# An order change at a stage border: the flip of token tile 15 directly behind that of tile 14, the first right side's differences and parts ahead of the second sums

## The chip, the cores and the metric

The kernel runs on one core of one Trainium2 chip. The metric is device time in microseconds (us), the median of several executions. Smaller is better.

## What is computed

A transformer block with adaptive layer norm, one sequence of 2048 tokens, width 512, all in float32:

```python
mod = (_silu(c) @ w_mod).reshape(c.shape[0], 6, 1, -1)
sa, ca, ga, sb, cb, gb = (mod[:, 0], mod[:, 1], mod[:, 2], mod[:, 3], mod[:, 4], mod[:, 5])
h = _layernorm(x, axis=-1) * (1 + ca) + sa
x = x + ga * _A_ref(h, A_wqkv, A_wo)
h = _layernorm(x, axis=-1) * (1 + cb) + sb
x = x + gb * _B_ref(h, B_w_gate, B_w_up, B_w_down)
```

`_A_ref` is linear attention with 32 heads of 16. `_B_ref` is a feed-forward part, `((x @ w_gate) * (x @ w_up)) @ w_down`, with 1376 hidden columns, worked on in 11 tiles of up to 128.

## The kernel before, in words

**Precision.** Each matmul operand is split into a high part (a ScalarE copy to fp32r) and a low part (the operand minus its high part, on VectorE or GpSimd). A product is three matmuls: high by high, high by low, low by high (`product` L205, `times` L1021). So every operand has to pass two engines before TensorE can use both of its parts.

**Tiles.** The 2048 tokens are 16 token tiles of 128 rows, in four chunks of four. In the attention's last part, `y_a(i)` (L748) multiplies the transposed queries of tile i with the output weights in 12 matmuls, on top of a residual that `y_seed(i)` (L740) has put into the accumulator bank `acc`, and `y_b(i)` (L757) takes the bank out on ScalarE (L763) and measures its mean and variance on VectorE (L229, L230). Two accumulator banks take turns (`y_bank`), so the seed of tile 15 waits for the statistics of tile 13.

Tiles 8 to 15 are transposed on the way through DRAM: `move_out` and `move_in` (DMA L709, L717) shift whole blocks, and `turn_v(i)` (L719) flips the 32x32 blocks on VectorE (L722, "the flip"). `turn_h(i)` (L674) makes the high part on ScalarE (L676), `turn_l(i)` (L678) the low part on VectorE (L680).

**The second stage.** The larger part of the feed-forward work uses a recursive product with seven half-size products in place of eight. For two chunks and one column tile, `block` (L1044) issues the seven products `times` of six matmuls each, into four banks a, b, c, d. In the order of TensorE: a = a11·b11; ScalarE copies a to b (`copy(b, a)`, L1031); d = s1·t1; b += s2·t2; a += a12·b21; ScalarE copies b to c; c += s3·t3; d += s4·b22; c += a22·t4. Here the left sides are token data: sums and differences s1 to s4 (`Left.sum`, L944 on GpSimd), split by `Left.split` (high L196 on ScalarE, low L197 on VectorE), once for each of k = 0 and k = 1 (`first[0]`, `first[1]`). The right sides are weights: `right_sums` makes the four differences t1 to t4 (L994), `right_split` makes the high parts on ScalarE (L1005 for b11, then L1008 for t1 and t2 together, for t3 and t4, for b21 and b22) and the low parts on GpSimd (L1012, in the same order).

**What sets the order.** Nothing reorders the program. `manual_schedule` keeps each engine's queue as the calls stand in the source, so every engine works through its list and waits in place for what its next instruction needs. SBUF tiles come out of a pool of 94 buffers; a new tile may wait for the last user of the buffer that it gets.

**The border between the stages.** The calls that the change moves stand at L1317 to L1332. Before them GpSimd makes the sums of `first[1]`. Behind them the first block begins: `work = ffn()`, then `y_step(14)` issues `y_a(14)`; `fill(1)` issues the first piece of block 0 (a and the copy); `y_b(14)`, `right_sums(1)` on VectorE and the splits of s3, s4 follow between the pieces d, and b and a; then comes `y_step(15)` with `y_a(15)`. `take()` is the adding of the last `down` pass to the residual (L824 on VectorE, twice).

Of the kernel before, what the change touches and what calls it, by code (L numbers as in the profile page):

```python
# [24 lines left out]
def tile_adaln_block(  # L25
# [12 lines left out]
    nc = tc.nc  # L38
# [31 lines left out]
    def f32(ap):  # L70
        return ap.bitcast(F32)
# [7 lines left out]
    def B(tag, shape=(P, D), dt=F32):  # L79

        return T(tiles, tag, shape, dt)
# [4 lines left out]
    def bank():  # L86
        return T(ps_w, "bank")
# [586 lines left out]
    def turn_h(i):  # L674
        pqs[i] = (B("xh", dt=F32R), B("xl", dt=F32R))
        nc.scalar.activation(pqs[i][0], tps[i], AF.Copy)  # L676

    def turn_l(i):  # L678
        h, l = pqs[i]
        nc.vector.tensor_tensor(l, tps.pop(i), f32(h), op=ALU.subtract)  # L680
# [38 lines left out]
    def turn_v(i):  # L719

        tps[i] = B("f")
        nc.vector.transpose(tps[i].rearrange("p (s m i) -> p m s i", m=NQ, i=BL),  # L722
                            moved.pop(i).rearrange("p (m i s) -> p m s i", m=NQ, i=BL))
# [16 lines left out]
    def y_seed(i, of=acc_bank):  # L740

        yps[i] = of()
        if of is bank:

            nc.tensor.matmul(yps[i], wp[0][0][:, :P], wp[0][0], start=True, stop=True)
        nc.scalar.activation(yps[i], xts[i // NJ][i % NJ], AF.Copy)
# [10 lines left out]
    def y_b(i):  # L757
        ch, j = divmod(i, NJ)
        ps = yps.pop(i)
        if ch in SUMS:  # L760
            norm2[ch].stats_act(j, ps)
            return
        nc.scalar.activation(xts[ch][j], ps, AF.Copy)  # L763
        norm2[ch].stats(j, of=ps)
# [372 lines left out]
    def right_sums(n, on=None):  # L1137
        if n < len(steps):
            rights[n].sums(on)

    def right_split(n, on=None):
        if n < len(steps):
            rights[n].high()
            rights[n].lows(on)
# [3 lines left out]
    def draw_load(n):  # L1148
        if n < len(steps):
            f0, k = fts[steps[n][1]]  # L1150
            draws[n] = load(w_down[f0:f0 + k, :], "raw")

    banks = []
# [120 lines left out]
    first = [Left((0, 1), k).into(side) for k in range(KH)]  # L1274
# [42 lines left out]
    first[1].sum("s1", "s3", "s2", "s4", on=nc.gpsimd)  # L1317
    y_seed(14, y_bank)
    turn_h(14)
    first[0].split("s1", "s2")  # L1320
    turn_l(14)
    y_b(13)
    y_seed(15, y_bank)
    right_sums(0, nc.vector)
    take()
    first[1].split("s1", "s2")
    turn_v(15)
    for n in range(4):
        banks.append(bank())
    banks[:] = [banks[n] for n in (2, 0, 1, 3)]  # L1330
    turn_bank[0] = acc_bank
    right_split(0)  # L1332
    draw_load(0)
    stash, second_side, plan = {}, {}, {}
    work = ffn()
# [79 lines left out]
```

## Time and profile before

| | before |
|---|---|
| median of 3 runs | 560.55 us (558.2, 560.55, 560.79) |
| the profiled execution's own time | 559.39 us |
| its span, first to last instruction | 557.7 us |
| granted TensorE clock, mean | 0.997 |
| TensorE busy | 550.1 us of the span |
| VectorE, ScalarE, GpSimd busy | 377.8, 291.4, 203.0 us |

The durations of the sections below come from the profiled execution. Its own time is 1.7 us above its span. In the timeline rows the columns are start, duration (of the whole run of equal neighbours), engine, source line, operation, output<-input, count, and in brackets the idle time of the engine ahead of it with what ended it. PE is TensorE, PEld its weight loads, DVE VectorE, ACT ScalarE, POOL GpSimd.

### The profile page before, as it was taken

How to read it: one execution, taken by the hardware profiler on the slowest of the kernel's cores; microseconds unless marked ns; L12 is line 12 of the kernel's file. 1: busy time of each engine (PE TensorE's matmuls, PEld its weight loads, DVE VectorE, ACT ScalarE, POOL GpSimd, SP SyncE). 2: the span in 40 equal slices, each digit the busy share in tenths (PEclk: the TensorE clock that was granted, in tenths of full speed). 3: DMA queues.
4: the chain of work that ended last, by engine and by line, in shares of the span. 5: the costliest groups of instructions: out<-in, count | busy, mean ns of one | idle time of the engine just before them, and what ended most of it. 6: DMA issues, size and time to landing. Idle time of an engine off the chain costs nothing.

```text
span 557.7 us, 7356 instructions
## 1 busy us (share of the span) xinstructions
PE 550.1 (99%) x2505; PEld 451.3 (81%) x2505; DVE 377.8 (68%) x605; ACT 291.4 (52%) x539; POOL 203.0 (36%) x203
## 2 busy tenths in 40 slices
PE   8999999999999999999899999999999999999997
PEld 6888888888888878878688888887888888888886
DVE  7896968977947886877877587886553544434435
ACT  3695856646477567566683545554444444444110
POOL 2000000101012300055698666566667446446200
PEclk9899999999999999999999999999999999999999
DMA  8900203220532605846435162591335222100004
GB/s 279 384 16 2 75 25 103 101 76 1 155 100 92 188 20 169 264 143 162 132 75 148 42 201 65 188 318 29 113 114 150 59 56 58 56 21 0 1 0 150
DMA packets 59141, 60.39 MB, mean 108 GB/s; under 512 B 8608, under 2 KB 37536, under 8 KB 59104
## 3 DMA queue, kind: packets, MB, share of 16 engines
q1 hardware_dynamic: 59104, 59.93, 34.3%
q8 instruction: 19, 0.31, 0.2%
q14 instruction: 18, 0.15, 0.1%
HBM read 43.65 MB, written 16.26 MB: 107 GB/s over the span
## 4 chain that ended last, share of the span: by engine, by line
PE 92%; DVE 3%; ACT 2%; DMA 1%; issue 1%; SPq 0%; DVEq 0%; ACTq 0%
PE bank L1026 32%; PE acc L1106 6%; PE acc L1107 6%; PE acc L1108 6%; PE acc L755 5%; PE bank L209 5%; PE bank L211 5%; PE bank L210 5%; PE acc L351 3%; PE acc L349 3%; PE acc L350 3%; PE bank L839 2%; PE bank L837 2%; PE bank L838 2%; PE bank L272 2%; DMA x<-in_A_x_dram 1%
## 5 line engine op out<-in xcount | busy, mean ns | idle before, releaser
L1026 PE MATMUL bank<-h,w 128*128 128x512 f32 (+1 forms) x798 | 185.4, 390 | 1.5 <-ACT bank L1031 1.5
L1026 PEld LDWEIGHTS bank<-h,w 128*128 128x128 f32 (+1 forms) x798 | 148.1, 186 | 35.8 <-ACT bank L1031 2.6
L1031 ACT ACTIVATE bank<-bank 128x512 f32<-128x512 f32 (+1 forms) x38 | 22.1, 583 | 137.1 <-PE bank L1026 137.0
L824 DVE TENSOR_TENSOR x<-acc,x 128x512 f32<-128x512 f32 (+1 forms) x73 | 48.4, 681 | 47.4 <-PE acc L1108 47.3
L1012 POOL TENSOR_TENSOR w<-raw,w 128x256 fp32r<-128x256 f32 (+3 forms) x38 | 41.3, 1086 | 95.2 <-ACT w L1005 95.2
L1107 PE MATMUL acc<-w,kh 128*128 128x512 f32 (+2 forms) x154 | 59.6, 387 | 0.0
L1106 PE MATMUL acc<-w,kh 128*128 128x512 f32 (+2 forms) x154 | 59.6, 387 | 0.0
L1108 PE MATMUL acc<-w,kl 128*128 128x512 f32 (+2 forms) x154 | 59.5, 386 | 0.0
L197 POOL TENSOR_TENSOR w<-raw,w 128x512 fp32r<-128x512 f32 (+1 forms) x25 | 36.0, 1442 | 55.3 <-ACT w L196 28.5
L250 POOL TENSOR_TENSOR rstd<-ve,half 128x4 f32<-128x4 f32 (+1 forms) x10 | 10.8, 1080 | 120.7 <-DVE ve L249 68.0
L1012 POOL TENSOR_TENSOR w<-t,w 128x512 fp32r<-128x512 f32 (+1 forms) x38 | 49.3, 1320 | 0.0
L197 DVE TENSOR_TENSOR kl<-u,kh 128x512 fp32r<-128x512 f32 (+1 forms) x38 | 26.4, 733 | 30.2 <-ACT kh L196 30.2
L209 PE MATMUL bank<-w,h 128*128 128x512 f32 x104 | 40.8, 392 | 0.0
L211 PE MATMUL bank<-w,h 128*128 128x512 f32 x104 | 40.5, 390 | 0.0
L210 PE MATMUL bank<-w,h 128*128 128x512 f32 x104 | 40.5, 389 | 0.0
L755 PE MATMUL acc<-w,xh 128*128 128x512 f32 x120 | 37.7, 395 | 0.0
L1106 PEld LDWEIGHTS acc<-w,kh 128*128 128x128 f32 (+1 forms) x154 | 28.9, 188 | 6.0
L1108 PEld LDWEIGHTS acc<-w,kl 128*128 128x128 f32 (+1 forms) x154 | 28.9, 188 | 5.9
L1107 PEld LDWEIGHTS acc<-w,kh 128*128 128x128 f32 (+1 forms) x154 | 28.9, 188 | 5.9
L1085 DVE TENSOR_TENSOR u<-bank,u 128x512 f32<-128x512 f32 (+1 forms) x19 | 13.1, 687 | 28.9 <-PE bank L1026 22.9
L259 ACT ACTIVATE n<-x,nmr,rstd 128x512 f32<-128x512 f32 x30 | 22.9, 804 | 12.2 <-DVE nmr L254 12.2
L196 ACT ACTIVATE w<-raw 128x512 fp32r<-128x512 f32 (+2 forms) x44 | 26.3, 619 | 1.9 <-DVE raw L804 1.0
(206 smaller groups left out, 1125.1 us busy)
## 6 DMA issues: line engine op xcount, KB each, us to landing
raw<-in_w_mod_dram SPq DMA_DIRECT2D x24, 256.0 KB, 3.8
raw<-in_B_w_down_dram SPq DMA_DIRECT2D x20, 256.0 KB, 3.2
raw<-in_B_w_gate_dram SPq DMA_DIRECT2D x36, 128.0 KB, 3.7
raw<-in_B_w_up_dram SPq DMA_DIRECT2D x36, 128.0 KB, 3.6
x<-in_A_x_dram SPq DMA_DIRECT2D x16, 256.0 KB, 5.7
out_dram<-x SPq DMA_DIRECT2D x15, 256.0 KB, 2.6
raw<-in_A_wqkv_dram SPq DMA_DIRECT2D x12, 256.0 KB, 5.4
wp<-w SPq DMA_DIRECT2D x8, 256.0 KB, 3.3
```

Of the source, the lines that this page charges most:

```text
L196: nc.scalar.activation(h, src, AF.Copy)
L197: (low or nc.vector).tensor_tensor(l, src, f32(h), op=ALU.subtract)
L209: nc.tensor.matmul(ps, ah, bh, start=i == 0, stop=False)
L210: nc.tensor.matmul(ps, ah, bl, start=False, stop=False)
L211: nc.tensor.matmul(ps, al, bh, start=False, stop=i == n - 1)
L755: nc.tensor.matmul(yps[i], x, y, start=False, stop=k == KD - 1 and x is al, skip_group_check=True)
L824: nc.vector.tensor_tensor(xt[:, a:b], dn[j][:, a:b], xt[:, a:b], op=ALU.add)
L1012: sub = lambda out, x, y: (on or nc.gpsimd).tensor_tensor(out, x, f32(y), op=ALU.subtract)
L1026: mm = lambda x, y, **kw: nc.tensor.matmul(ps, x[:, k], y, skip_group_check=True, **kw)
L1106: nc.tensor.matmul(ps, hh[:, a:b], dh[:n, c:d], start=i == 0, stop=False)
L1107: nc.tensor.matmul(ps, hh[:, a:b], dl[:n, c:d], start=False, stop=False)
L1108: nc.tensor.matmul(ps, hl[:, a:b], dh[:n, c:d], start=False, stop=i == len(hs) - 1)
```

## The change

The calls between the last seed and the first block stand in another order. The flip of tile 15 goes directly behind that of tile 14, followed on VectorE by the four differences of the first right side. The high part of tile 15 goes ahead of the exit of tile 13. The splits of s1 and s2 of `first[0]` move behind the seed of tile 15; `right_split(0)` moves between them and the splits of `first[1]`. `take()` and the low part of tile 15 come behind these. The line that gave the four banks a, b, c, d in the order 2, 0, 1, 3 is gone, so they are taken in the order of allocation.

```diff
     y_seed(14, y_bank)
     turn_h(14)
-    first[0].split("s1", "s2")
+    turn_v(15)
+    right_sums(0, nc.vector)
     turn_l(14)
+    turn_h(15)
     y_b(13)
     y_seed(15, y_bank)
-    right_sums(0, nc.vector)
+    first[0].split("s1", "s2")
+    right_split(0)
+    first[1].split("s1", "s2")
     take()
-    first[1].split("s1", "s2")
-    turn_v(15)
+    turn_l(15)
     for n in range(4):
         banks.append(bank())
-    banks[:] = [banks[n] for n in (2, 0, 1, 3)]
     turn_bank[0] = acc_bank
-    right_split(0)
     draw_load(0)
     stash, second_side, plan = {}, {}, {}
     work = ffn()
```

No instruction is added or taken away. The order of the instructions on TensorE, GpSimd and the DMA queue (SP) is the same in both programs; on ScalarE and VectorE it differs at this border alone.

## The prediction

> **What bounds the kernel now.** First the page: the busy shares, the chain that ended last, and the costliest group.
>
> ```profile
> PE 550.1 (99%) x2505; PEld 451.3 (81%) x2505; DVE 377.8 (68%) x605; ACT 291.4 (52%) x539; POOL 203.0 (36%) x203
> ...
> PE 92%; DVE 3%; ACT 2%; DMA 1%; issue 1%; SPq 0%; DVEq 0%; ACTq 0%
> ...
> L1026 PE MATMUL bank<-h,w 128*128 128x512 f32 (+1 forms) x798 | 185.4, 390 | 1.5 <-ACT bank L1031 1.5
> ```
>
> TensorE sets the time, so an order change can only win what TensorE waits for. The second stage (L1026) has one such wait of size, 1.5 us for the ScalarE copy L1031. The timeline of TensorE places it, in block 0, directly behind the moved calls; the rows of the weight loads name a second, smaller one.
>
> ```profile
> 263.59 3.19 PE L1026 MATMUL bank<-h,w 128*128 128x512 f32 x12
> 268.29 3.02 PE L1026 MATMUL bank<-h,w 128*128 128x512 f32 x12 [1.51 <-ACT bank L1031]
> 271.15 0.61 PE L755 MATMUL acc<-w,xh 128*128 128x512 f32 x2
> ...
> 273.87 16.48 PE L1026 MATMUL bank<-h,w 128*128 128x512 f32 x72
> ```
> ```profile
> 265.59 0.76 PEld L1026 LDWEIGHTS bank<-h,w 128*128 128x128 f32 x4 [0.43 <-POOL w L1012]
> 268.29 0.53 PEld L1026 LDWEIGHTS bank<-h,w 128*128 128x128 f32 x3 [1.95 <-ACT bank L1031]
> ```
>
> The undisturbed pace is the row at 273.87: (16.48 - 0.39)/71 = 0.2266 us per matmul. From 263.59, 24 matmuls should bring the tile's next product to 263.59 + 24 x 0.2266 = 269.03. It starts at 271.15. So **2.12 us** are lost here, and that is the ceiling of the gain. They fall into about 0.3 (GpSimd's low part of t1, t2) and 1.8 (the copy and the restart).
>
> Why is the copy late? ScalarE:
>
> ```profile
> 257.24 0.63 ACT L676 ACTIVATE xh<-f 128x512 fp32r<-128x512 f32 x1 [0.71 <-DVE f L722]
> 257.77 1.14 ACT L196 ACTIVATE h<-s 128x512 fp32r<-128x512 f32 x2
> 258.81 0.58 ACT L763 ACTIVATE x<-acc 128x512 f32<-128x512 f32 x1
> 260.96 0.60 ACT L746 ACTIVATE acc<-x 128x512 f32<-128x512 f32 x1 [1.57 <-DVE st L229]
> 261.50 1.14 ACT L196 ACTIVATE h<-s 128x512 fp32r<-128x512 f32 x2
> 262.54 0.40 ACT L1005 ACTIVATE w<-raw 128x256 fp32r<-128x256 f32 x1
> 262.85 1.14 ACT L1008 ACTIVATE w<-t 128x512 fp32r<-128x512 f32 x2
> 263.89 0.62 ACT L1008 ACTIVATE w<-raw 128x512 fp32r<-128x512 f32 x1
> 267.12 0.63 ACT L676 ACTIVATE xh<-f 128x512 fp32r<-128x512 f32 x1 [2.61 <-DVE f L722]
> 267.66 0.58 ACT L1031 ACTIVATE bank<-bank 128x512 f32<-128x512 f32 x1
> ```
>
> The copy (267.66) stands behind the high part of tile 15 (267.12), for which ScalarE idles 2.61 us until VectorE flips that tile. VectorE:
>
> ```profile
> 256.10 1.10 DVE L722 STREAM_TRANSPOSE f<-u 128x512 f32<-128x512 f32 x1
> 258.42 1.29 DVE L197 TENSOR_TENSOR h<-s,h 128x512 fp32r<-128x512 f32 x2 [1.22 <-ACT h L196]
> 259.63 0.69 DVE L680 TENSOR_TENSOR xl<-f,xh 128x512 fp32r<-128x512 f32 x1
> 260.24 0.69 DVE L229 BATCH_NORM_STATS2 st<-acc 128x6 f32<-128x512 f32 x1
> ...
> 261.06 0.39 DVE L994 TENSOR_TENSOR t<-raw 128x256 f32<-128x256 f32 x1
> ...
> 262.50 1.28 DVE L824 TENSOR_TENSOR x<-acc,x 128x512 f32<-128x512 f32 x2
> 263.70 2.38 DVE L197 TENSOR_TENSOR h<-s,h 128x512 fp32r<-128x512 f32 x2
> 266.00 1.08 DVE L722 STREAM_TRANSPOSE f<-u 128x512 f32<-128x512 f32 x1
> 267.78 1.22 DVE L680 TENSOR_TENSOR xl<-f,xh 128x512 fp32r<-128x512 f32 x1 [0.69 <-ACT xh L676]
> ...
> 269.74 0.39 DVE L994 TENSOR_TENSOR t<-raw 128x256 f32<-128x256 f32 x1
> ...
> 271.19 2.49 DVE L197 TENSOR_TENSOR h<-s,h 128x512 fp32r<-128x512 f32 x4
> ```
>
> **The change, part by part.** Nothing is added; the counts and shapes stay. I follow each queue from 256.10, with starts taken from neighbouring rows.
>
> *VectorE, first half.* The second flip fills the idle 1.22 us: 257.15 to 258.2. The four L994 take 262.50 - 261.06 = 1.44, so 258.1 to 259.6. The low part of tile 14 follows until 260.2, the statistics of tile 13 start at 260.15 (before: 260.24). The added wait is the flip's wait for its fetch; behind it stand the L994, the low part of tile 14 and, through the statistics, the seed of tile 15. Its cost I put at nothing:
>
> ```profile
> 245.13 5.69 SPq L717 DMA_DIRECT2D u<-moved  x12
> ```
> ```profile
> DMA to landing us min/median/max: 2.0/2.3/4.0
> ```
>
> The first row is SP's issue of the fetches, the second the landing of this tile's transfers (u). The last fetch is issued by 250.8 and at 4.0 lands before 255. TensorE needs the low part of tile 14 for the third matmul of `y_a(14)`, at 263.59 - 10 x 0.2266 = 261.3: 1.1 us to spare.
>
> *ScalarE.* High part of tile 15 at 258.25, exit of tile 13 at 258.8 as before, seed of tile 15 at 260.9. Then, at the starts' distances of the rows (0.54, 2 x 0.52, 0.31, 3 x 0.52, 2 x 0.52), s1 and s2 of `first[0]` from 261.4, b11 at 262.5, the three L1008 from 262.8, s1 and s2 of `first[1]` at 264.35 and 264.85, **the copy from 265.4 to 266.0**. TensorE reaches its reader at 263.59 + 12 x 0.2266 = 266.3. The 1.8 us of the copy go, with 0.3 to spare.
>
> *What is late next: GpSimd.* Its list is unchanged, four L1012.
>
> ```profile
> 263.02 0.74 POOL L1012 TENSOR_TENSOR w<-raw,w 128x256 fp32r<-128x256 f32 x1 [6.41 <-ACT w L1005]
> ...
> 267.19 1.27 POOL L1012 TENSOR_TENSOR w<-raw,w 128x512 fp32r<-128x512 f32 x1
> 273.18 1.70 POOL L1012 TENSOR_TENSOR w<-raw,w 128x256 fp32r<-128x256 f32 x1 [4.73 <-ACT w L1005]
> 274.85 2.54 POOL L1012 TENSOR_TENSOR w<-t,w 128x512 fp32r<-128x512 f32 x2
> ```
> ```profile
> 263.73 1.81 POOL L1012 TENSOR_TENSOR w<-t,w 128x512 fp32r<-128x512 f32 x1
> ```
> ```profile
> 264.30 1.78 DVE L197 TENSOR_TENSOR h<-s,h 128x512 fp32r<-128x512 f32 x1
> ```
>
> The last part (low of b21, b22) ended at 267.19 + 1.27 = 268.46. Undisturbed, TensorE now wants it for its 21st matmul, at 263.59 + 20 x 0.2266 = 268.12. And L1012 and L197 do not run beside each other: the L1012 at 263.73 takes 1.81 where those at 274.85 take 1.27, and the L197 at 264.30 takes 1.78 where the pair at 258.42 takes 0.65 each, ending 0.55 behind that L1012. The L824 beside the L1012 of 263.02 keep 0.64 and 0.74. So L197 and L680 take turns with L1012, L824 doesn't. By turns, VectorE's s2 of `first[0]` runs 262.7 to 263.3; b11's low part waits for it, 263.3 to 264.0 (wanted at 264.04: under 0.1 lost); t1, t2 until 265.3 (wanted at 265.4); s1 of `first[1]` until 265.95; t3, t4 until 267.2; s2 of `first[1]` until 267.85; b21, b22 until **269.1**, 1.0 behind the wish. Then the low part of tile 15 until 269.75, statistics and L994 as at 268.93 to 271.19 (2.3), and the third of the four L197 (s3 of `first[1]`) until 273.85. TensorE wants that one for its 41st matmul, at 263.59 + 40 x 0.2266 = 272.65. That makes the loss 1.2. The gain is 2.1 - 1.2 = **0.9 us**.
>
> [...]
>
> *Tiles and banks.* The order of allocation puts some tiles on other buffers; their new predecessors (fetches of tiles 12 to 15, old parts) were all done over 1 us before they are wanted. SP's list does not change, and its next needed loads are for later blocks. The banks a to d become other banks, in all blocks. No row shows what a bank's place costs. Nearest row:
>
> ```profile
> L1026 PE MATMUL bank<-h,w x798: 387/389/501, 263.6 to 534.6; 128*128 128x512 f32 x189, 128*96 128x512 f32 x11
> ```
>
> Below, 798 matmuls from the mean of 390 to the least, 387 ns, would be 2.4 us; above I set the same, an estimate by symmetry. I take nothing, because the median of 389 lies at the least. Past 273.87 no TensorE wait is shown, so the gain is kept to the end.
>
> **Sum.** The profiled execution has 559.39 us (span 557.7): 558.5 (556.8) after. The median of the runs shown is 1.16 above it, at 560.55, so the time predicted is 560.55 - 0.9 = 559.6.
>
> **The rivals.**
>
> 1. *VectorE keeps its turn* (as at 273.18): s2 of `first[1]` goes directly behind s1, t3 and t4 end at 267.8, the low part of tile 15 goes ahead of b21, b22, which end at 269.7: loss 1.6, gain 0.5, 560.0. For it the 1.70; against it the 1.81 and 1.78, where turns were taken.
> 2. *The whole wait goes.* Four L1012 without a block take 0.74 + 3 x 1.27 and end at 262.95 + 4.55 = 267.5, ahead of the wish at 268.12. Gain up to 2.1, 558.4. Against it: four instructions of VectorE fall into that stretch.
> 3. *Nothing moves*: b21, b22 or the third L197 come so late that all is given back (from 270.2 or 274.75 on): 560.55.
> 4. *Slower: the head of VectorE's queue slides.* The flip of tile 15 now stands ahead of the L994, the low part of tile 14, the statistics and so the seed; should its blocks land late, everything slides with them. The 0.9 are used up when the seed is 0.9 late, thus from a landing at 258.05; at 260 the kernel is 1.95 slower, 562.5. Against it: the landing before 255.
> 5. *The banks' place tells* over all blocks, to either side by up to 2.4: 557.2 to 562.0 with the forecast.
>
> **How the numbers follow.** Forecast (gain 0.6 to 1.5) 0.50; rival 1: 0.14; rival 2: 0.20; rival 3: 0.07; rival 4: 0.03; rival 5: 0.03 to each side. A measurement of this kernel tells about 0.5%, 2.8 us, from no change. No case with a row reaches that, but the three runs shown lie 2.6 apart: I give a quarter of rival 2, a twentieth of the forecast and most of rival 5's good side to faster, 0.10; the bad side of rival 5, part of rivals 3 and 4 to slower, 0.05; 0.85 remain. The range: 2.1 off the median and 1.2 for the runs' spread give 557.2; no gain and the spread upwards 561.3.
>
> **What would show it.** Right: no wait of TensorE for L1031 in block 0, ScalarE idle before L676 of tile 15 under 0.3 us, the copy ahead of 266.4; a new wait of TensorE for POOL L1012 of some 0.3 to 1.0 and perhaps for DVE L197; the row that was at 273.87 now at about 273.0. Wrong: the copy still named; no wait for L1012 (then rival 2); the seed of tile 15 after 261.3 (then rival 4); L1026's mean other than 390 (then rival 5).

## The result and the profile after

| | before | after |
|---|---|---|
| median, 6 runs each | 559.35 us (558.2 to 560.79) | 562.86 us (562.41 to 564.67) |
| ratio of the runs to before | | 1.0068, interval 1.0045 to 1.009 |
| the profiled execution, its span | 559.39, 557.7 us | 562.92, 561.2 us |

The kernel became 3.5 us slower. The page of after, the share of TensorE and its group of the second stage (idle time and its end in the last column):

```profile
PE 552.1 (98%) x2505; PEld 451.6 (80%) x2505; DVE 381.3 (68%) x605; ACT 291.6 (52%) x539; POOL 203.2 (36%) x203
...
L1026 PE MATMUL bank<-h,w 128*128 128x512 f32 (+1 forms) x798 | 187.9, 393 | 3.5 <-DVE h L197 3.3
```

The wait for the copy L1031 is gone, as forecast. In its place stands a longer one, for VectorE's low parts (L197). TensorE's timeline of after:

```profile
262.58 6.29 PE L1026 MATMUL bank<-h,w 128*128 128x512 f32 x24
...
271.46 0.39 PE L1026 MATMUL bank<-h,w 128*128 128x512 f32 x1
272.81 0.98 PE L1026 MATMUL bank<-h,w 128*128 128x512 f32 x3 [0.96 <-DVE h L197]
276.16 24.62 PE L1026 MATMUL bank<-h,w 128*128 128x512 f32 x98 [2.38 <-DVE h L197]
```

The first 24 matmuls of block 0 are now one run. Those of c += s3·t3 stop twice: at the second, which reads the low part of s3 for k = 0, and at the fifth, for k = 1. What comes next is slow as well. Two stretches of after; the columns are the length, the busy time and count of instructions of TensorE, its weight loads, VectorE, ScalarE and GpSimd, then TensorE's granted clock, the share of the DMA engines and GB/s:

```profile
271.40:276.10 4.70, 1.42 (x5) 0.51 (x4) 4.70 (x4) 0.84 (x2) 4.16 (x3) 1.00 0.59 161
276.10:281.00 4.90, 4.84 (x14) 3.84 (x15) 3.31 (x7) 1.11 (x2) 1.28 (x1) 0.65 0.01 2
```

In the first, TensorE works 1.42 of 4.70 us while VectorE (4.70) is full and GpSimd (4.16) nearly so. In the second the granted clock is 0.65: 14 matmuls where 4.9 us would hold 21, at 0.2266 us each.

The sum can be read from one stretch, blocks 0 to 2 with tile 15's product between, from the first matmul to the end of the last. The last row of before, up to the end of block 2:

```profile
273.87 23.38 PE L1026 MATMUL bank<-h,w 128*128 128x512 f32 x102
```

Before, the stretch is 273.87 + 23.38 - 263.59 = 33.66 us, after 276.16 + 24.62 - 262.58 = 38.20: 4.5 us lost. The spans differ by 3.5 alone because block 0 began 1.0 us earlier in the profiled execution of after; that comes from the kernel's first microseconds, which the change does not touch (last section). The medians depend on the granted clock too: of 58 further runs of before, those with a mean clock of 0.999 or 1.0 took 558.1 to 559.3 us, and those at 0.993 or 0.994 took 560.6 to 561.2.

Why is L197 late? VectorE and GpSimd of after:

```profile
263.96 2.48 DVE L197 TENSOR_TENSOR h<-s,h 128x512 fp32r<-128x512 f32 x2 [1.62 <-ACT h L196]
...
268.99 0.39 DVE L994 TENSOR_TENSOR t<-raw 128x256 f32<-128x256 f32 x1
...
270.10 0.96 DVE L994 TENSOR_TENSOR t<-raw,t 128x256 f32<-128x256 f32 x1
270.98 5.73 DVE L197 TENSOR_TENSOR h<-s,h 128x512 fp32r<-128x512 f32 x4
```
```profile
270.98 1.77 DVE L197 TENSOR_TENSOR h<-s,h 128x512 fp32r<-128x512 f32 x1
```
```profile
265.86 1.75 POOL L1012 TENSOR_TENSOR w<-raw,w 128x512 fp32r<-128x512 f32 x1
269.89 0.89 POOL L1012 TENSOR_TENSOR w<-raw,w 128x256 fp32r<-128x256 f32 x1 [2.29 <-ACT w L1005]
270.74 3.15 POOL L1012 TENSOR_TENSOR w<-t,w 128x512 fp32r<-128x512 f32 x2
273.86 1.71 POOL L1012 TENSOR_TENSOR w<-raw,w 128x512 fp32r<-128x512 f32 x1
```

The four L197 of s3, s4 took 2.49 us before and take 5.73 now: the first three 1.77, 1.76 and 1.75 (the single row is the first), and the last, with no L1012 beside it any more, 0.68. So a row's duration holds the wait as well, some 1.1 us here. Beside the first three runs GpSimd's next round of L1012, the low parts of the *second* right side. Before, that round began at 273.18, when the four were all but done. It hangs on ScalarE's L1005, and ScalarE no longer loses 2.61 us waiting for the flip:

```profile
264.36 0.57 ACT L1031 ACTIVATE bank<-bank 128x512 f32<-128x512 f32 x1
...
269.40 0.41 ACT L1005 ACTIVATE w<-raw 128x256 fp32r<-128x256 f32 x1
```

So the engine that was freed set off work that collides with the next work on TensorE's path. (The four L197 also start 0.8 us later behind block 0's start than before; e6 shows that this second shift is needed too.) That is theory 1, "turns". The rivals tested: the other place of the banks (theory 2), and a list on VectorE that is too long at this place with or without GpSimd (theory 3).

### The profile page after: what moved, and what is told of

Same layout as the page of the kernel before. It is cut to its first block, busy times and chain, and to the rows that moved or that the text cites. A ratio compares the mean times of both kernels' runs of the same rounds, so it can differ in the third digit from the quotient of the medians.

```text
span 561.2 us, 7354 instructions
## 1 busy us (share of the span) xinstructions
PE 552.1 (98%) x2505; PEld 451.6 (80%) x2505; DVE 381.3 (68%) x605; ACT 291.6 (52%) x539; POOL 203.2 (36%) x203
## 4 chain that ended last, share of the span: by engine, by line
PE 89%; DVE 5%; ACT 3%; DMA 1%; issue 1%; SPq 0%; DVEq 0%; ACTq 0%
PE bank L1026 29%; PE acc L1106 6%; PE acc L1107 6%; PE acc L1108 6%; PE acc L755 5%; PE bank L209 5%; PE bank L211 5%; PE bank L210 5%; PE acc L351 3%; PE acc L350 3%; PE acc L349 3%; PE acc L148 2%; PE bank L839 2%; PE bank L838 2%; PE bank L837 2%; PE bank L272 2%
## 5 line engine op out<-in xcount | busy, mean ns | idle before, releaser
L1026 PE MATMUL bank<-h,w 128*128 128x512 f32 (+1 forms) x798 | 187.9, 393 | 3.5 <-DVE h L197 3.3
L1026 PEld LDWEIGHTS bank<-h,w 128*128 128x128 f32 (+1 forms) x798 | 148.9, 188 | 39.5 <-DVE h L197 4.7
L1031 ACT ACTIVATE bank<-bank 128x512 f32<-128x512 f32 (+1 forms) x38 | 22.1, 583 | 137.5 <-PE bank L1026 137.5
L824 DVE TENSOR_TENSOR x<-acc,x 128x512 f32<-128x512 f32 (+1 forms) x73 | 48.4, 680 | 47.4 <-PE acc L1108 47.3
L1012 POOL TENSOR_TENSOR w<-raw,w 128x256 fp32r<-128x256 f32 (+3 forms) x38 | 41.6, 1096 | 94.2 <-ACT w L1005 94.2
L197 POOL TENSOR_TENSOR w<-raw,w 128x512 fp32r<-128x512 f32 (+1 forms) x25 | 35.5, 1423 | 57.8 <-ACT w L196 31.1
L1012 POOL TENSOR_TENSOR w<-t,w 128x512 fp32r<-128x512 f32 (+1 forms) x38 | 49.4, 1324 | 0.0
L197 DVE TENSOR_TENSOR kl<-u,kh 128x512 fp32r<-128x512 f32 (+1 forms) x38 | 27.1, 754 | 31.6 <-ACT kh L196 31.6
L1085 DVE TENSOR_TENSOR u<-bank,u 128x512 f32<-128x512 f32 (+1 forms) x19 | 13.1, 687 | 27.2 <-PE bank L1026 21.1
```

What stands on the lines that cost most here:

```text
L197: (low or nc.vector).tensor_tensor(l, src, f32(h), op=ALU.subtract)
L824: nc.vector.tensor_tensor(xt[:, a:b], dn[j][:, a:b], xt[:, a:b], op=ALU.add)
L1012: sub = lambda out, x, y: (on or nc.gpsimd).tensor_tensor(out, x, f32(y), op=ALU.subtract)
L1026: mm = lambda x, y, **kw: nc.tensor.matmul(ps, x[:, k], y, skip_group_check=True, **kw)
```

## The experiments

The table has one row per kernel. The time is the median; the ratio is to runs of the kernel before. e1 to e4 ran on one chip and e5 to e8 on another, beside 29 runs of before each, with medians of 558.67 and 559.22 us; so differences from after are given by the ratios. "Three blocks" is the stretch above; L197 is the duration of the four low parts of s3 and s4.

| kernel | time, us | ratio, interval | three blocks | L197 |
|---|---|---|---|---|
| before | 559.35 | | 33.66 | 2.49 |
| after | 562.86 | 1.0068 (1.0045 to 1.009) | 38.20 | 5.73 |
| e1 s3, s4 on GpSimd | 559.2 | 1.0011 (1.0002 to 1.0019) | 34.09 | on GpSimd, 6.14 |
| e2 second right side on VectorE | 558.28 | 0.9991 (0.9979 to 1.0002) | 33.29 | 2.49 |
| e3 banks alone | 558.76 | 1.0003 (0.9991 to 1.0015) | 33.65 | 2.49 |
| e4 TensorE kept busy | 561.1 | 1.0042 (1.003 to 1.0054) | 36.48 | 5.78 |
| e5 differences later | 558.23 | 0.9977 (0.9962 to 0.9991) | 33.04 | 3.01 |
| e6 flip alone | 559.21 | 0.9996 (0.9983 to 1.0009) | 33.90 | 4.13 |
| e7 flip, differences later | 558.0 | 0.9976 (0.9962 to 0.9989) | 32.48 | 2.76 |
| e8 GpSimd beside | 566.57 | 1.0127 (1.0105 to 1.015) | 41.44 | 6.24 |

**e1: s3 and s4 go to GpSimd.** From after:

```diff
-    first[0].split("s3", "s4")
+    first[0].split("s3", "s4", low=nc.gpsimd)
     fill(1)
-    first[1].split("s3", "s4")
+    first[1].split("s3", "s4", low=nc.gpsimd)
```

> The changed kernel, but the low parts of s3 and s4 of both k are made by GpSimd, ahead of the second right side's parts, not by VectorE beside them. Theory 1 (turns): in the changed kernel the four L197 of s3, s4 take 1.75 us each because GpSimd's L1012 of the second right side now run beside them, and TensorE's two waits (1.1 and 2.5 us) and the half clock after them come from that; here both waits go, and the time is some 4 us below the changed kernel and 0.5 to 1.5 below before: 558.0 to 559.0. Theory 2 (the banks' other place in all blocks): as the changed kernel, 562 to 563. Theory 3 (VectorE's list is too long at this place, with or without GpSimd): the waits shrink as well, since VectorE is relieved of 2.5 us; it can't be told from theory 1 here.

3.2 us of the loss go by the ratios, but the kernel ends 0.1% above before, where theory 1 had it 0.5 to 1.5 us below. The collision has moved: GpSimd now runs beside VectorE's L994. VectorE, GpSimd, and TensorE's waits of e1:

```profile
272.20 1.51 DVE L994 TENSOR_TENSOR t<-raw,raw 128x256 f32<-128x256 f32 x1
273.64 1.51 DVE L994 TENSOR_TENSOR t<-raw,t 128x256 f32<-128x256 f32 x1
```
```profile
268.73 6.14 POOL L197 TENSOR_TENSOR h<-s,h 128x512 fp32r<-128x512 f32 x4
```
```profile
PE bank L1026 <- DVE u L1085: 1.3, 1, 1.3
```

An L994 of 0.42 us takes 1.51 there, and the L1085 behind it on VectorE makes TensorE wait 1.3 us.

**e2: GpSimd silent, VectorE with more to do.** From after; the second right side's low parts alone go to VectorE:

```diff
-                      ... lambda: right_split(m + 1)],
+                      ... lambda: right_split(m + 1, nc.vector if m == 0 else None)],
```

> The changed kernel, but the low parts of the second right side alone are made by VectorE, behind the four L197 of s3, s4, so that GpSimd is silent beside them. Theory 1 (turns): the L197 take 0.61 to 0.69 each, the wait for the first goes, that for the third is at most 0.5, no half clock; some 3 to 4 us below the changed kernel, 558.5 to 560. Theory 2 (banks): as the changed kernel. Theory 3 (VectorE's list too long by itself): VectorE has more to do, not less, and the waits stay at 1 us or more each.

VectorE and TensorE of e2:

```profile
270.55 2.49 DVE L197 TENSOR_TENSOR h<-s,h 128x512 fp32r<-128x512 f32 x4
```
```profile
262.70 6.28 PE L1026 MATMUL bank<-h,w 128*128 128x512 f32 x24
271.55 24.44 PE L1026 MATMUL bank<-h,w 128*128 128x512 f32 x102
```

The L197 are back at 0.62 each although VectorE has four instructions more (they stand behind the L197), and TensorE doesn't stop. This decides against theory 3. The time is slightly under the band expected, and 4.3 us below after by the ratios.

**e3: the banks alone.** From before, the line `banks[:] = [banks[n] for n in (2, 0, 1, 3)]` is taken out.

> The kernel before, without the line that reorders the four banks; nothing else is moved. Theory 1: as before, within 0.5 us. Theory 2 (banks): the whole 3.5 us appear here, about 562.9, spread over all blocks.

The old wait is unchanged in its timeline, and the time is that of before. Theory 2 falls.

```profile
268.06 3.03 PE L1026 MATMUL bank<-h,w 128*128 128x512 f32 x12 [1.49 <-ACT bank L1031]
```

**e4: TensorE kept busy.** From after; the extra matmuls' results are not used:

```diff
-    todo = []
+    todo, filled = [], []
...
+        if not filled:
+            filled.append(True)
+            for _ in range(16):
+                nc.tensor.matmul(a, wp4[0][0][:, :P], wp4[0][0], start=True, stop=True)
         times(c, A["s3"], R["t3"], False)
```

> The changed kernel with 16 extra matmuls (3.6 us at 0.2266 each) into the free bank a, ahead of the product that waits for s3; they compute nothing that is used. They fill TensorE's wait and take no wait away. If the half clock behind the wait comes from TensorE's idling, the matmuls behind it keep 0.227 us and the kernel is 1.3 to 1.9 us below the changed one, about 561.2. If the half clock has another cause (a die's throttle, a slot in time), it stays, and the time is the changed kernel's, 562.9, or up to 0.3 above.

TensorE's timeline of e4, and the stretch 276 to 281:

```profile
271.28 3.79 PE L1087 MATMUL bank<-w 128*128 128x512 f32 x16
274.91 24.01 PE L1026 MATMUL bank<-h,w 128*128 128x512 f32 x102
```
```profile
276.00:281.00 5.00, 4.92 (x21) 4.02 (x22) 4.35 (x10) 1.12 (x2) 1.32 (x2) 1.00 0.16 48
```

With the L197 as slow as in after (5.78), and 3.8 us of useless work, the kernel is 1.5 us faster than after by the ratios, and its three blocks are 38.20 - 36.48 = 1.7 us shorter. The clock stays at 1.00. So some 1.7 of the 4.5 us were the half clock, as after's second stretch says by itself ((1 - 0.65) x 4.90 = 1.7), and it came from TensorE's own idling.

**e5: the second side's differences later.** From after:

```diff
-    right_sums(1, nc.vector)
     first[0].split("s3", "s4")
     fill(1)
     first[1].split("s3", "s4")
+    right_sums(1, nc.vector)
     fill(2)
```

> The changed kernel, with the four differences of the second right side behind the splits of s3 and s4 on VectorE, not ahead of them. The L197 of s3, s4 then start some 1.5 us earlier, and GpSimd's L1012 for t1 to t4 of the second right side wait for those differences, so that VectorE meets only GpSimd's first, short L1012 there. Theory 1 (turns): the L197 take 0.65 each but for one; no wait of TensorE over 0.4 us at s3, no half clock; 557.0 to 558.3, and at least 0.5 below before. Theory 3 (VectorE's list too long by itself) expects the same sign and a gain of only the 1.5 us on the changed kernel, 561 to 561.5.

Theory 1 is met in sign and size (the median lies inside its band), theory 3's 561 to 561.5 is not. VectorE and GpSimd of e5:

```profile
269.13 3.01 DVE L197 TENSOR_TENSOR h<-s,h 128x512 fp32r<-128x512 f32 x4
```
```profile
270.01 0.97 POOL L1012 TENSOR_TENSOR w<-raw,w 128x256 fp32r<-128x256 f32 x1 [2.27 <-ACT w L1005]
```

One short L1012 falls into the four L197. The long ones wait for the differences: the first, the low parts of t1 and t2, starts at 273.68 after 2.69 us of idling, 0.75 us behind the end of the L994 that makes t2 (272.51 + 0.42).

**e6: the flip alone.** From before:

```diff
     turn_h(14)
+    turn_v(15)
     first[0].split("s1", "s2")
     turn_l(14)
+    turn_h(15)
     y_b(13)
...
     first[1].split("s1", "s2")
-    turn_v(15)
+    turn_l(15)
```

> The kernel before, with one part of the change: the flip of tile 15 behind that of tile 14 and its high part ahead of the exit of tile 13. Theory 1 (turns): this part alone removes the wait for the copy, lets ScalarE run ahead and so brings GpSimd's next L1012 beside the L197 of s3, s4: the waits of TensorE at s3 appear as in the changed kernel, 1 to 4 us in all, and the time is 0 to 3.5 us above before. If the loss came from the moved differences and parts of the first right side, this kernel would be faster than before by 1 to 2 us.

No gain, no loss: the copy's wait has gone, and is given back. The gain of 1 to 2 us that would have put the whole loss on the moved differences doesn't come either. TensorE, VectorE and GpSimd of e6:

```profile
269.87 1.20 PE L1026 MATMUL bank<-h,w 128*128 128x512 f32 x4 [0.36 <-POOL w L1012]
...
277.63 20.73 PE L1026 MATMUL bank<-h,w 128*128 128x512 f32 x90 [1.13 <-DVE u L1085]
```
```profile
271.14 4.13 DVE L197 TENSOR_TENSOR h<-s,h 128x512 fp32r<-128x512 f32 x4
```
```profile
272.08 0.95 POOL L1012 TENSOR_TENSOR w<-raw,w 128x256 fp32r<-128x256 f32 x1 [2.27 <-ACT w L1005]
```

GpSimd's round starts 0.94 us behind the first L197, in after 1.09 us ahead of it. Here the four take 1.64 us more than before (4.13 against 2.49), beside the short L1012 and the first of the long ones, and the L1171 behind them takes 1.77 beside the next. The waits for s3 itself that I expected do not come, but VectorE falls behind and L1085 is late by 1.13.

These rows also say where the full loss comes from. Counted from the start of block 0, GpSimd's round starts at 9.59 us before, at 7.62 in e6 and at 7.31 in after; the first L197 starts at 7.60, 6.68 and 8.40. So the early flip alone brings GpSimd's round 2.0 us forward, and the rest of the change puts the four L197 1.7 us later than in e6, beside the three long L1012 of that round. The full loss takes both.

**e7: the flip, and the differences later.** e6 with the edit of e5.

> The kernel of the early flip alone, and the differences of the second right side behind the splits of s3 and s4. Theory 1 (turns): the copy's wait is gone and the L197 of s3, s4 have VectorE to themselves; 1.0 to 2.0 us below before. Without theory 1 the second edit does nothing: as the early flip alone.

This has the lowest time of the kernels run. By its ratio it is 1.3 us under before, inside the expected 1.0 to 2.0, and it beats both kernels. Its TensorE has one wait left in this place:

```profile
268.42 1.20 PE L1026 MATMUL bank<-h,w 128*128 128x512 f32 x4 [0.39 <-POOL w L1012]
272.19 23.30 PE L1026 MATMUL bank<-h,w 128*128 128x512 f32 x102
```

e5 (558.23) and e7 (558.0) have overlapping intervals; which of them is better stays open.

**e8: the collision without the change.** From before, in its old order; the five subtractions are not used:

```diff
     right_split(0)
+    spare = B("u")
+    for _ in range(5):
+        nc.gpsimd.tensor_tensor(spare, first[0].f["s1"], first[1].f["s1"], op=ALU.subtract)
     draw_load(0)
```

> The kernel before in its old order, with five extra subtractions of 128x512 on GpSimd behind the first right side's parts; nothing uses them. They put GpSimd beside VectorE's L994 and L197 of s3, s4 and move nothing else. Theory 1 (turns): the four L994 take some 5 us in place of 1.44, the L197 1.75 each, TensorE waits at s3 for 1 to 5 us and may fall to the half clock: 560.5 to 567. Theory 3: VectorE's list has not changed, nothing happens, within 0.5 us of before.

GpSimd, VectorE and TensorE of e8:

```profile
267.81 7.46 POOL L1335 TENSOR_TENSOR u<-s,s 128x512 f32<-128x512 f32 x5
```
```profile
274.07 6.24 DVE L197 TENSOR_TENSOR h<-s,h 128x512 fp32r<-128x512 f32 x4
```
```profile
275.88 0.96 PE L1026 MATMUL bank<-h,w 128*128 128x512 f32 x3 [2.21 <-DVE h L197]
278.69 3.78 PE L1026 MATMUL bank<-h,w 128*128 128x512 f32 x8 [1.84 <-DVE h L197]
```

The picture of after, its two waits and slow matmuls behind them, appears in the old order once GpSimd has work there: the eight from 278.69 take 3.78 us, where the undisturbed pace gives 7 x 0.2266 + 0.39 = 1.98. The four L994, from 269.15 to 274.07, take 4.9 us in place of 1.44, as expected. (The extra work also makes the second right side's parts later, so the 7 us are not the price of the turns alone.)

## Why the prediction was wrong

The forecast was a gain of 0.9 us; measured is a loss of 3.5, outside the range of 557.2 to 561.3, with 0.05 given to its side. Step by step, with the 1.0 us added to after's times by which its block 0 began earlier ("moved" below):

- **VectorE's first half and ScalarE: right.** The copy was forecast to start at 265.4; it starts at 264.36, moved 265.4. The wait for it has gone.
- **GpSimd's first round: right in kind, a little large in size.** b21, b22 were forecast to end at 269.1; they end at 265.86 + 1.75 = 267.61, moved 268.6. The loss of the first 24 matmuls was put at 1.0; tile 15's product follows in after at 271.46 - 12 x 0.2266 = 268.74, against 262.58 + 24 x 0.2266 = 268.02: 0.7. The forecast had a wait of TensorE for L1012; no row of its matmuls names one, but its weight loads do, with waits of 0.22 and 0.39 us, and one of 0.45 for an L197 between them.
- **The step that failed is "statistics and L994 as at 268.93 to 271.19 (2.3), and the third of the four L197 until 273.85".** The four were to start at 269.75 + (271.19 - 268.93) = 272.0; they start at 270.98, moved 272.0. The place was exact, the duration was not: I took some 0.61 us each from the row at 271.19, where GpSimd was silent for nearly all of them, and they take 5.73 in all. The matmul that waits for the third starts at 276.16, moved 277.2, 3.3 us behind the forecast.
- **What was left out behind it:** I worked out that ScalarE is early, and did not follow what it issues next. With the copy done 2.3 us earlier against its block (267.66 - 263.59 before, 264.36 - 262.58 after), everything behind it on ScalarE moves up, the L1005 of the second right side with it, and with that GpSimd's next round. I left that where the old trace has it, at 273.18. The two halves of the collision were both in my text, as rows.
- **The half clock, some 1.7 us,** was no term at all. Without it the time would have been about 561.2, at the upper edge of the range, and e4, which keeps the full clock, took 561.1: still a loss where a gain was forecast.
- **Rivals.** Rival 3 named "the third L197" and a point, 274.75, but no mechanism that reaches it, and it stopped at no gain. Rival 4, the only slower one, did not happen: the seed of tile 15 came at 259.87, moved 260.9, as forecast. Rival 5: its sign shows, a mean of L1026 of 393 ns in place of 390, but e3, with the banks alone, has the time of before (ratio 1.0003), and nine of after's matmuls from 276.73 to 280.54, at the half clock, take up to 628 ns each (median 628) in place of 389, together some 2 us of the 2.5 by which the group grew (187.9 - 185.4); so most of that sign comes from the half clock. Rival 1 and the alternation: among the L197 and L1012 of after the two engines took strict turns, as in the forecast (from 272 on the rows end at 272.21, 273.90 and 275.57 on GpSimd, at 272.75, 274.44 and 276.11 on VectorE).
- **The baseline and the range.** The forecast of 559.6 stood on a median of 560.55 from three runs; six gave 559.35. The range's upper end of 561.3 is 0.75 above that 560.55, where the lower end allows 1.2 for the spread; with 1.2 it would be 561.75, and the 562.86 would still lie above it.
- **The turns were the right mechanism, used one round too short.** Four L197 beside three L1012 cost 3.2 us more: each of the first three takes some 1.1 us longer (1.77 against 0.69), where an L1012 with no L197 beside it takes 1.29 (before, 274.85).

## What to carry to other kernels

When an edit removes a wait on an engine, list what that engine issues next until the next point where it waits anyway, and lay every one of those, on all engines that they set off, over the new times; a duration from the old trace holds only with the old neighbours. VectorE and GpSimd operations that lengthen each other in a trace are to be counted as taking turns, as L197 (1.77 us against 0.69, beside L1012) and L994 (1.51 against 0.42, beside GpSimd's L197) did here; L824, which adds a bank to x, kept 0.68 us beside an L1012 (266.37 in after). Where two such runs must pass the same place, a cheap cure is to let the one that is not urgent wait for data that comes later (here the differences), so that it starts behind the other.

## What the runs showed of the hardware

In after, TensorE's granted clock fell to half for a stretch behind two waits. Before, e3 and e6 have single waits of 1.51, 1.49 and 1.13 us in block 0 and keep their pace: the 12, 12 and 90 matmuls behind them start 0.24, 0.24 and 0.23 us apart. After has 0.96 and 2.38 us with three matmuls between, e8 2.21 and 1.84, and both slow down behind them: in after matmuls start 0.43 us apart (276.96, 277.38, 277.81), in e8 (3.78 - 0.39)/7 = 0.48. After's granted clock is 0.98 from 276.1 to 277.0, 0.50 from 277.0 to 280.4 and 1.00 from there to 281.0, so it fell some 0.8 us behind the end of the second wait (276.16). For e8 there is the mean clock of whole runs alone, 0.99 to 0.993, against 0.993 to 1.0 of before beside it. So in these runs two waits of 3.34 us (after) and 4.05 us (e8) in all went with the slow matmuls, and a single one of 1.51 did not; whether it has to be two waits, and from which length of idling on, is not shown, as no run has a single wait in block 0 of a length in between.

The 1.0 us at the kernel's start comes with a half clock too. The same early stretch in the profiled execution of before, then of after, the granted clock third from the end:

```profile
15.70:19.10 3.40, 3.40 (x9) 2.57 (x9) 2.66 (x9) 3.40 (x7) 0.00 (x0) 0.50 1.05 388
```
```profile
15.70:19.10 3.40, 3.40 (x16) 2.57 (x15) 2.66 (x8) 3.40 (x7) 0.00 (x0) 1.00 1.05 388
```

Nine matmuls against sixteen, in code that the change does not touch. In before TensorE is busy for 5.47 of the 5.70 us ahead of it, so idling as in block 0 doesn't explain it; why it comes in one execution and not in the other stays open.
